# The last 96 rows of an FFN product in 32-row tiles of the array, four token tiles at a time

## The chip, the cores and the metric

The kernel runs on one core of a Trainium2 chip. A core has a matrix engine (TensorE, PE in the profile; its weight loads are listed apart as PEld), three elementwise engines (VectorE or DVE, ScalarE or ACT, GpSimd or POOL) and SyncE (SP), which here only issues DMAs. The engines run side by side and wait for each other by semaphores; each takes its own instructions in the order in which they were written. Matrix products go to PSUM, eight banks of 128 partitions by 512 float32 columns. The metric is the device time of one execution in microseconds, the median of several runs; a profile shows one execution.

## The reference

For 2048 tokens of width 512 the output is a gated sum of two branches:

```python
g = sigmoid((x * gate_w).sum(-1, keepdims=True))
return g * A(x) + (1 - g) * B(x)
# A: q, k, v = x @ wqkv in 32 heads of 16;  pq = q @ w_phi, pk = k @ w_phi, head by head
#    phi(p) = concat(softmax(p), softmax(-p))
#    kv = sum_s phi_k^T v,  z = sum_s phi_k;  o = (phi_q kv) / (phi_q z);  A = o @ wo
# B: relu(x @ w1) @ w2, inner width 1376
```

The inner width 1376 is ten blocks of 128 and a remainder of 96. The change is about that remainder.

## The kernel before, in words

The 2048 tokens are 16 tiles `m` of 128 (NT), or four chunks `c` of 512. All instructions are added as named tasks with their dependencies, and the strings in `ORDER` (line 17) fix by hand the order in which each engine runs its tasks. A task waits until its dependencies are done, and what stands behind it on its engine waits with it. Figures such as `dur` and `boost` in the code belong to a planner and set nothing here.

The tasks that matter:

- `h{c}_{k}` (line 391): first FFN product for chunk c and hidden block k, written transposed (hidden rows, token columns); `rl{c}_{k}` on ScalarE applies ReLU and writes it into `HT` (line 469). For the remainder, k = 10, `h{c}_10` (line 399) computes 97 columns for each of four token tiles, tokens in rows: 96 hidden columns and the gate's product. `rl{c}_10` writes the 96 into `HR` (line 452), and a DMA transpose `hx{c}` on SP brings four blocks of 128 by 128 into `HT` (line 454). `hpad` (line 251) clears the columns 96 to 127.
- `f1_{j}`, `fe1_{j}`, j = 0 to 3: the feature map folded into the key projection's weights, on TensorE, and its copy out of PSUM, on VectorE (j even) and ScalarE (j odd).
- `pr_k0` to `pr_k8`, then `pr_q0` to `pr_q8` (line 512): key and query projections into PSUM banks 0 and 1, two token tiles at a time (the last two of each kind one). Each is followed by a chain through the elementwise engines: `ev` (copy, ScalarE), `mx` and `mn` (VectorE), `t1` and `t2` (GpSimd), `ex` (exponential, ScalarE), `sm` and `rc` (sum and reciprocal, VectorE), `ra` and `nm` (GpSimd).
- `v{m}`, `kv{m}`: values and the sums over keys. `kn`, `kz`: the masked copies of those sums.
- `tq{m}`: DMA transpose of the normalised query features. `nd{m}_0`, `nd{m}_1` (line 616): four small matmuls each, numerator and denominator of tile m, into bank 6 and bank 7. `rd{m}_*` and `o{m}_*` (lines 623, 625): reciprocal and quotient on VectorE; an `o` frees the bank, so `nd2_0` waits for `o1_0`. `to{m}`: DMA transpose of the quotient.
- `b{m}` (line 638): the second FFN product of tile m, eleven matmuls of 512 columns into one of the banks 3, 4, 5, 2 (`AB`, tile m takes the entry m modulo 4), the last with 96 rows. It leaves the accumulation open. `a{m}` (line 644): four matmuls with `wo` that end it. The quotient was scaled by exp of the gate's sum, so that one factor 1 - g serves both.
- `oe{m}` (line 689): multiplies by 1 - g and copies out of PSUM, on ScalarE; it frees the bank for `b{m+4}`. `st{m}`: the store, from ScalarE's queue. Tile 15 is computed in two column parts, `b15` (line 659) for both, then `a15_0`, `a15_1` (line 670), with copies on ScalarE (line 677) and VectorE (line 680).

The loads stand at the head of SP's queue: `w2a` and `w2b` are the ten full blocks of `w2` and its last 96 rows, `wo` the output weights.

Of the kernel before, what the change touches and what calls it, by code (L numbers as in the profile page):

```python
# [5 lines left out]
ACT = mybir.ActivationFunctionType  # L6
ALU = mybir.AluOpType
# [14 lines left out]
    ),  # L22
# [15 lines left out]
    ),  # L38
# [11 lines left out]
    ),  # L50
# [10 lines left out]
    ),  # L61
# [87 lines left out]
def bass_gated_mix__linear_kernel_hedgehog__dense_activation_relu__prompt_kernel(  # L149
# [32 lines left out]
    NDB, AB = (6, 7), (3, 4, 5, 2)  # L182
    GATE_LIMIT = 40.0
    WARM = (6 * (512,),)
    RL = 400.0
    FE = "dve"

    with ExitStack() as es:
        E = es.enter_context

        def sb(name, shape, dt):
            return E(nc.sbuf_tensor(name, shape, dt))

        XT = sb("XT", [P, ND, S], BF16)
        HT = sb("HT", [P, KT, S], BF16)
        WT = sb("WT", [P, 2 * ND, D], BF16)
        WP = sb("WP", [P, 2, ND, D], BF16)
        WV = sb("WV", [P, ND, D], BF16)
        W1 = sb("W1", [P, ND, W1C], BF16)
        W2 = sb("W2", [P, KT, D], BF16)  # L200
        WO = sb("WO", [P, ND, D], BF16)
        WPS = sb("WPS", [P, ND, DH], BF16)
# [30 lines left out]
        EPS = 8 * 512  # L233

        def ap(t, row, off, dims):
            return bass.AP(tensor=t, offset=off, ap=[[row, P]] + [list(d) for d in dims])

        def psap(off, dims):
# [11 lines left out]
            ap(VS, NT * NG * GZ, GV, [[GZ, NT * NG], [1, 1]]), 1.0), dur=0.7, boost=-1e4)  # L250
        add("hpad", "pool", lambda q: q.memset(HR[:, :, :, KREM:P], 0.0), dur=0.6, boost=-1e4)
        XN = FT[:, NF - 2, :].rearrange("p (m d) -> p m d", d=D)
# [61 lines left out]
        load("w2a", "sp", W2[:, 0:KT - 1, :], B_w2[0:(KT - 1) * P, :].rearrange("(j p) n -> p j n", p=P), dur=0.5, lat=8.0)  # L314
        load("w2b", "sp", W2[0:KREM, KT - 1, :], B_w2[(KT - 1) * P:DFF, :], dur=0.5, lat=8.0)
        load("wo", "sp", WO[:, :, :], A_wo.rearrange("(j p) n -> p j n", p=P), dur=0.5, lat=8.0)

# [124 lines left out]
        for n, (kind, a, k) in enumerate(units):  # L442
            b = GB4[n] if n < 4 else FB[2] if n == 4 else HB[(n - 4) % len(HB)]
            if kind == "h":
                halved = n < 4
                deps = [*xof[a], *w1of[k], prev, *freed[b]]
                if k == KT - 1:
                    deps.append("gw")
                    add(f"h{a}_{k}", "pe", lambda q, a=a, b=b: pe_h_tail(q, a, b), deps, dur=0.69)
                    prev = f"h{a}_{k}"  # L450
                    hrow = psap(b * 512, [[KREM + 1, 4], [1, KREM]])
                    add(f"rl{a}_{k}", "act", lambda q, a=a, i=hrow: q.activation(
                        HR[:, a % 2, :, 0:KREM], i, ACT.Relu), (prev, f"hx{a - 2}" if a > 1 else None), dur=0.6, boost=RL)
                    add(f"hx{a}", "sp", lambda q, a=a: q.dma_start_transpose(
                        out=HT[:, KT - 1, chunk(a)].rearrange("p (n t) -> p n t", t=P),
                        in_=HR[:, a % 2, :, :].rearrange("p n k -> p (n k)")),
                        (f"rl{a}_{k}", "hpad"), dur=1.2, lat=1.6, dma=True)
                    add(f"gr{a}", "dve", lambda q, a=a, b=b: q.tensor_scalar(
                        GL[:, 4 * a:4 * a + 4], psap(b * 512 + KREM, [[KREM + 1, 4]]), GATE_LIMIT, -GATE_LIMIT,
                        ALU.min, ALU.max), (prev, f"rl{a}_{k}"), dur=0.2, boost=500.0)  # L460
                    freed[b] = (f"rl{a}_{k}", f"gr{a}")
                    gate(a)
                    continue
# [32 lines left out]
        for m in range(NT):  # L496
            def add(*a, boost=20.0 * (len(widths) * 2 - m // 2 - VLAG), **how):
                return g.add(*a, boost=boost, **how)
# [9 lines left out]

        def pe_proj(q, s, tiles):
            for n, m in enumerate(tiles):  # L510
                for j in range(ND):
                    last = q.matmul(PS[:, n, :], XT[:, j, m * P:(m + 1) * P], WP[:, s, j, :],  # L512
                                    start=(j == 0), stop=(j == ND - 1))
            return last

        jname = []
        for jn, (kind, tiles) in enumerate(jobs):
# [15 lines left out]
            def old(x, J2=two):  # L533
                return f"{x}_{J2}" if J2 else None

            add(f"pr_{J}", "pe", lambda q, s=s, tiles=tiles: pe_proj(q, s, tiles),
                [*(f"fe{s}_{j}" for j in range(ND)), *(d for m in tiles for d in xof[m // 4]),
                 *([f"ev_{before}"] if before else ["fe1_0", "fe1_1"])], dur=0.87 * w)
# [40 lines left out]
            else:  # L579
# [29 lines left out]
                for m in tiles:  # L609
# [25 lines left out]
                    def pe_b(q, m=m, ab=ab):  # L635
                        for k in range(KT):
                            r = P if k < KT - 1 else KREM
                            last = q.matmul(PS[:, ab, :], HT[0:r, k, m * P:(m + 1) * P], W2[0:r, k, :],  # L638
                                            start=(k == 0), stop=False)
                        return last  # L640
# [8 lines left out]
                    if m == NT - 1:  # L649

                        hb = (ab, 0)
                        cols = [slice(0, 352), slice(352, D)]
                        last_b = f"b{m}"

                        def pe_bh(q, m=m, hb=hb, cols=cols):
                            for b, cs in zip(hb, cols):
                                for k in range(KT):
                                    r = P if k < KT - 1 else KREM
                                    last = q.matmul(PS[:, b, 0:cs.stop - cs.start], HT[0:r, k, m * P:(m + 1) * P], W2[0:r, k, cs],  # L659
                                                    start=(k == 0), stop=False)  # L660
                            return last

                        g.add(last_b, "pe", pe_bh, ("w2a", "w2b", *(f"rl{m // 4}_{k}" for k in range(KT - 1)), f"hx{m // 4}", *war,
                                                    f"ev_{J}"), dur=2.42)
                        for h2 in range(2):
                            b, cs = hb[h2], cols[h2]

# [5 lines left out]

                            add(f"a{m}_{h2}", "pe", pe_ah, (last_b, "wo", f"to{m}", f"a{m}_0" if h2 else None), dur=0.44)
                            need = (f"a{m}_{h2}", f"go{m // 4}", f"st{m - NOS}")
# [10 lines left out]
                        continue  # L686
                    g.add(f"b{m}", "pe", pe_b, ("w2a", "w2b", *(f"rl{m // 4}_{k}" for k in range(KT - 1)), f"hx{m // 4}", *war), dur=2.38)
                    add(f"a{m}", "pe", pe_a, (f"b{m}", "wo", f"to{m}"), dur=0.87)
                    add(f"oe{m}", "act", lambda q, m=m, ab=ab: q.activation(  # L689
                        OSB[:, m % NOS, :], PS[:, ab, :], ACT.Copy, scale=OMG[:, m:m + 1]),  # L690
                        (f"a{m}", f"go{m // 4}", f"st{m - NOS}" if m >= NOS else None), dur=0.69)
                    add(f"st{m}", "act", lambda q, m=m: q.dma_start(
                        out=o2[m * P:(m + 1) * P, :], in_=OSB[:, m % NOS, :]), (f"oe{m}",), dur=0.5, lat=1.5, dma=True)
# [44 lines left out]
```

## Time and profile before

| | us |
|---|---|
| median of 3 runs | 150.46 (150.14 to 150.74) |
| profiled execution | 150.59 |
| its span, first to last instruction | 149.3 |
| TensorE busy in it | 146.3 |
| VectorE, GpSimd, ScalarE busy | 110.9, 109.6, 91.8 |

TensorE's granted clock was 1.00 throughout. In the lists of the profile a group is a line of the kernel, an engine, an operation and its tiles (written <- read, buffer numbers left out), with the number of instructions, the time that the group keeps its engine busy, the mean of one in ns, and the engine's idle time just before them with what ended it. The chain in order of time gives start, length and the instructions that it follows. A timeline gives start, length from the first start to the last end, engine, line and shape, and the idle time ahead. W1 and W2 share the name W.

### The profile page before, as it was taken

The page shows a single profiled execution, that of the slowest core. Times are in us where ns is not written, and L with a number is a line of the kernel's source. Part 1 is how long each engine was busy: PE and PEld are TensorE (multiplying, and loading weights), DVE is VectorE, ACT ScalarE, POOL GpSimd, SP SyncE. Part 2 cuts the span into 40 slices and gives each one's busy share as a digit, 9 for nine tenths or more (in the row PEclk, how much of TensorE's full clock was granted, in tenths as well). Part 3 has the DMA queues.
Part 4 walks back from the last instruction along what each step waited for, and adds up shares of the span by engine and source line. Part 5 has one row for each costly group of instructions (what it writes and reads, how often), then busy time and mean ns, then how long its engine had stood idle before and what let it go on. Part 6 is the DMA issues. An engine that isn't in the chain of part 4 may idle for free.

```text
span 149.3 us, 2619 instructions
## 1 busy us (share of the span) xinstructions
PE 146.3 (98%) x1009; PEld 75.9 (51%) x1009; DVE 110.9 (74%) x168; ACT 91.8 (61%) x127; POOL 109.6 (73%) x72
## 2 busy tenths in 40 slices
PE   7999999999999999999999999999999999999994
PEld 2865444444754465445444545455444444445452
DVE  2343666999796948989999997999989988534401
ACT  3374769799979775898983937175573751310151
POOL 4000399999999999999999999999999793150000
PEclk9999999999999999999999999999999999999999
DMA  5999999900030001000000094646778687656552
GB/s 144 303 234 247 171 212 211 341 27 0 7 70 0 0 4 37 0 0 4 0 0 0 2 111 104 141 103 139 121 169 190 159 212 97 156 134 159 63 156 91
DMA packets 46364, 16.11 MB, mean 108 GB/s; under 512 B 39856, under 2 KB 46352, under 8 KB 46352
## 3 DMA queue, kind: packets, MB, share of 16 engines
q1 hardware_dynamic: 43616, 13.50, 43.2%
q10 hardware_dynamic: 2736, 2.45, 5.1%
q8 instruction: 8, 0.13, 0.4%
q14 instruction: 4, 0.03, 0.1%
HBM read 4.41 MB, written 2.10 MB: 44 GB/s over the span
## 4 chain that ended last, share of the span: by engine, by line
PE 98%; DVE 0%; issue 0%
PE PS L638 24%; PE PS L391 21%; PE PS L512 19%; PE PS L492 9%; PE PS L644 9%; PE PS L573 3%; PE PS L616 3%; PE PS L399 2%; PE PS L405 2%; PE PS L258 2%; PE PS L659 2%; PE PS L411 1%; PE PS L374 1%; PE PS L350 1%; PE PS L670 1%; DVE OSB L680 0%
## 5 line engine op out<-in xcount | busy, mean ns | idle before, releaser
L552 POOL TENSOR_TENSOR TS<-PB,MX 128x1024 bf16<-128x1024 bf16 (+1 forms) x18 | 30.9, 1723 | 15.0 <-DVE MX L543 15.0
L638 PE MATMUL PS<-W,HT 128*128 128x512 bf16 (+1 forms) x165 | 38.1, 379 | 0.0
L559 DVE TENSOR_REDUCE ZB<-FT 128x128 f32<-128x2048 bf16 (+1 forms) x18 | 36.6, 2031 | 1.8 <-ACT FT L557 1.8
L557 ACT ACTIVATE FT<-TS 128x2048 bf16<-128x2048 bf16 (+1 forms) x18 | 30.9, 1718 | 8.7 <-POOL TS L552 8.5
L391 PE MATMUL PS<-XT,W 128*128 128x512 bf16 x144 | 34.7, 379 | 0.0
L552 POOL TENSOR_TENSOR TS<-MN,PB 128x1024 bf16<-128x1024 bf16 (+1 forms) x18 | 30.9, 1725 | 0.8 <-DVE MN L545 0.8
L512 PE MATMUL PS<-WP,XT 128*128 128x512 bf16 x128 | 30.6, 379 | 0.0
L566 POOL TENSOR_TENSOR FT<-FT,SC 128x2048 bf16<-128x2048 bf16 (+1 forms) x9 | 29.5, 3287 | 0.0
L469 ACT ACTIVATE HT<-PS 128x512 bf16<-128x512 f32 x40 | 22.6, 597 | 5.6 <-PE PS L391 4.6
L638 PEld LDWEIGHTS PS<-W,HT 128*128 128x128 bf16 (+1 forms) x165 | 15.5, 98 | 17.1
L689 ACT ACTIVATE OSB<-PS,OMG 128x512 bf16<-128x512 f32 x15 | 10.2, 687 | 22.4 <-PE PS L644 22.3
L543 DVE TENSOR_REDUCE MX<-PB 128x64 bf16<-128x1024 bf16 (+1 forms) x18 | 19.5, 1084 | 6.0 <-ACT PB L539 6.0
L545 DVE TENSOR_REDUCE MN<-PB 128x64 bf16<-128x1024 bf16 (+1 forms) x18 | 19.3, 1084 | 3.2 <-ACT PB L539 3.2
L391 PEld LDWEIGHTS PS<-XT,W 128*128 128x128 bf16 x144 | 13.8, 98 | 15.3
L539 ACT ACTIVATE PB<-PS 128x1024 bf16<-128x1024 f32 (+1 forms) x18 | 16.7, 927 | 7.3 <-PE PS L512 4.2
L512 PEld LDWEIGHTS PS<-WP,XT 128*128 128x128 bf16 x128 | 12.0, 98 | 13.6 <-DVE WP L344 0.4
L492 PE MATMUL PS<-WV,XT 128*128 128x512 bf16 x64 | 16.4, 379 | 0.0
L589 POOL TENSOR_TENSOR FT<-FT,SR 128x1024 bf16<-128x1024 bf16 (+1 forms) x9 | 15.7, 1739 | 0.7
L644 PE MATMUL PS<-WO,OT 128*128 128x512 bf16 x60 | 14.7, 379 | 0.0
L625 DVE SCALAR_TENSOR_TENSOR OTM<-PS,EG,RD 128x256 bf16<-128x256 f32 x32 | 13.8, 463 | 0.4 <-DVE RD L623 0.2
L623 DVE RECIPROCAL RD<-PS 128x16 f32<-128x16 f32 x32 | 6.4, 232 | 9.0 <-PE PS L616 8.8
L501 ACT ACTIVATE VS<-PS 128x512 bf16<-128x512 f32 x16 | 9.6, 602 | 4.3 <-PE PS L492 4.3
(54 smaller groups left out, 106.0 us busy)
## 6 DMA issues: line engine op xcount, KB each, us to landing
out_dram<-OSB ACTq DMA_DIRECT2D x15, 128.0 KB, 2.1
W<-in_B_w_dram SPq DMA_DIRECT2D x1, 1280.0 KB, 6.9
W<-in_B_w_dram SPq DMA_DIRECT2D x1, 512.0 KB, 4.9
WV<-in_A_wqkv_dram SPq DMA_DIRECT2D x1, 512.0 KB, 4.7
WO<-in_A_wo_dram SPq DMA_DIRECT2D x1, 512.0 KB, 7.2
FT<-in_A_x_dram SPq DMA_DIRECT2D x3, 128.0 KB, 3.8
W<-in_B_w_dram SPq DMA_DIRECT2D x1, 352.0 KB, 3.9
W<-in_B_w_dram ACTq DMA_DIRECT2D x2, 128.0 KB, 3.7
```

What stands on the lines that cost most here:

```text
L391: last = q.matmul(PS[:, b, :], W1[:, j, k * P:(k + 1) * P], XT[:, j, chunk(c)], start=(j == 0), stop=(j == ND - 1))
L469: add(f"rl{a}_{k}", "act", lambda q, a=a, k=k, b=b: q.activation(HT[:, k, chunk(a)], PS[:, b, :], ACT.Relu), (prev,), dur=0.6, boost=RL)
L492: last = q.matmul(PS[:, 2, :], XT[:, j, m * P:(m + 1) * P], WV[:, j, :], start=(j == 0), stop=(j == ND - 1))
L512: last = q.matmul(PS[:, n, :], XT[:, j, m * P:(m + 1) * P], WP[:, s, j, :], start=(j == 0), stop=(j == ND - 1))
L543: add(f"mx_{J}", "dve", lambda q, sl=sl, w=w, i=pbg: q.tensor_reduce(MX[:, sl, 0:w * H], i, AX.X, ALU.max), (f"ev_{J}", old("t1")), dur=0. ...
L545: add(f"mn_{J}", "dve", lambda q, sl=sl, w=w, i=pbg: q.tensor_reduce(MN[:, sl, 0:w * H], i, AX.X, ALU.min), (f"ev_{J}", old("t2")), dur=0. ...
L552: add(f"{tn}_{J}", "pool", lambda q, o3=o3, a3=a3, b3=b3: q.tensor_tensor(o3, a3, b3, ALU.subtract), (f"{'mx' if sg == 0 else 'mn'}_{J}", ...
L557: add(f"ex_{J}", "act", lambda q, fs=fs, ts=ts, w=w: q.activation(FT[:, fs, 0:w * F], TS[:, ts, 0:w * F], ACT.Exp), (f"t1_{J}", f"t2_{J}", ...
L559: add(f"sm_{J}", "dve", lambda q, fs=fs, sl=sl, w=w: q.tensor_reduce(ZB[:, sl, 0:2 * w * H], FT[:, fs, 0:w * F].rearrange("p (g d) -> p g ...
L566: add(f"nm_{J}", "pool", lambda q, f3=f3, sl=sl, w=w: q.tensor_tensor(f3, f3, SC[:, sl, 0:2 * w * H].unsqueeze(2).to_broadcast([P, 2 * w * ...
L638: last = q.matmul(PS[:, ab, :], HT[0:r, k, m * P:(m + 1) * P], W2[0:r, k, :], start=(k == 0), stop=False)
L644: last = q.matmul(PS[:, ab, :], OT[:, m % NOT, t, :], WO[:, t, :], start=False, stop=(t == ND - 1))
```

## The change

For token tiles 0 to 11 the last 96 rows leave the eleven-matmul product, which becomes ten. They are computed for four token tiles at once: a pack `p{c}`, c = 0, 1, 2, has 3 x 4 matmuls, each with 32 rows of the array. Row tile r (partitions 32r to 32r+31) holds token tile 4c + r and writes that tile's own bank. For this, `rl{c}_10` writes the remainder interleaved, so that one transposed block holds 32 hidden rows of each of the four token tiles (three blocks for each chunk; chunk 3 keeps four blocks and the old form); they go to a new buffer `HX`. The last 96 rows of `w2` are loaded four times more, by `w2x0` to `w2x3`, once for each row tile, into `W2X`. The order is rewritten: a pack follows the `b` of its four tiles, and the `a` tasks follow the pack. `pr_k0` is parted: its first two matmuls, `pr_k0a`, wait for the first two folded weights alone. Tile 15's columns are parted 416 and 96 in place of 352 and 160, its two parts are separate tasks, and `a14` stands between them; `oe14` moves to VectorE, `st14` to SP.

The order on TensorE, from `b0` on, as far as it differs:

```diff
-b0 nd0_0 nd0_1 b3 nd1_0 nd1_1 b2 pr_q6 a0 nd2_0 nd2_1 b1 nd3_1 pr_q7 nd3_0 b4 ...
+b0 nd0_0 nd0_1 b3 nd1_0 nd1_1 b2 pr_q6 nd2_0 nd2_1 b1 p0 a0 nd3_1 pr_q7 nd3_0 b4 ...
-b5 nd6_0 nd6_1 b7 nd7_0 nd7_1 a4 a5 b6 nd8_1 nd8_0 a6 b9 ...
+b5 nd6_0 nd6_1 b7 nd7_0 nd7_1 b6 p1 a4 a5 nd8_1 nd8_0 a6 b9 ...
-b10 nd11_1 a8 nd11_0 a9 b11 a10 nd12_0 nd12_1 b13 ...
+b10 nd11_1 nd11_0 b11 p2 a8 a9 a10 nd12_0 nd12_1 b13 ...
-a11 a12 a13 a14 b15 a15_0 a15_1
+a11 a12 a13 b15_0 a14 a15_0 b15_1 a15_1
```

On the other queues: SP has `w2x0 w2x1 w2x2 w2x3` between `w2b` and `wo`, and `st14` ahead of `st15_1`; ScalarE has `oe4` (with `oe5`, `oe6` behind it) after `ex_q6 gp2` in place of before `oe5 ge2 st2 ex_q6 gp2`, and no `oe14` and `st14`; VectorE has `oe14` between `o15_1` and `oe15_1`. VectorE's and GpSimd's orders are otherwise the same. The code, cut to its core:

```diff
+    NR = KREM // 32
-        HT = sb("HT", [P, KT, S], BF16)
+        HT = sb("HT", [P, KT - 1, S], BF16)
+        HX = sb("HX", [P, NC, 4 * P], BF16)
+        W2X = sb("W2X", [P, NR, D], BF16)
+        def ht(r, k, m):
+            if k == KT - 1:
+                return HX[0:r, m // 4, (m % 4) * P:(m % 4 + 1) * P]
+            return HT[0:r, k, m * P:(m + 1) * P]
...
-        add("hpad", "pool", lambda q: q.memset(HR[:, :, :, KREM:P], 0.0), dur=0.6, boost=-1e4)
+        add("hpad", "pool", lambda q: q.memset(HR[:, 1, :, KREM:P], 0.0), dur=0.6, boost=-1e4)
...
+        for n in range(4):
+            load(f"w2x{n}", "sp", W2X[32 * n:32 * n + 32, :, :], B_w2[(KT - 1) * P:DFF, :].rearrange("(f p) n -> p f n", p=32),
+                 dur=0.5, lat=8.0)
...
+                    nb = NR if a < NC - 1 else 4
+                    if nb == NR:
+                        hi = psap(b * 512, [[KREM + 1, 4], [32, NR], [1, 32]])
+                        ho = ap(HR, 8 * P, (a % 2) * 4 * P, [[32, 4], [P, NR], [1, 32]])
+                    else:
+                        hi = psap(b * 512, [[KREM + 1, 4], [1, KREM]])
+                        ho = HR[:, a % 2, :, 0:KREM]
+                    add(f"rl{a}_{k}", "act", lambda q, o=ho, i=hi: q.activation(o, i, ACT.Relu),
+                        (prev, "hpad", f"hx{a - 2}" if a > 1 else None), dur=0.6, boost=RL)
+                    add(f"hx{a}", "sp", lambda q, a=a, nb=nb: q.dma_start_transpose(
+                        out=HX[:, a, 0:nb * P].rearrange("p (n t) -> p n t", t=P),
+                        in_=HR[:, a % 2, 0:nb, :].rearrange("p n k -> p (n k)")),
...
+            steps = [(n2, m, j) for n2, m in enumerate(tiles) for j in range(ND)]
+            if jn == 0:
+                add(f"pr_{J}a", "pe", lambda q, s=s, steps=steps[:2]: pe_proj(q, s, steps),
+                    [f"fe{s}_0", f"fe{s}_1", *xof[0]], dur=0.44)
+                steps = steps[2:]
...
-                        for k in range(KT):
+                        for k in range(KT if m >= 12 else KT - 1):
                             r = P if k < KT - 1 else KREM
-                            last = q.matmul(PS[:, ab, :], HT[0:r, k, m * P:(m + 1) * P], W2[0:r, k, :],
+                            last = q.matmul(PS[:, ab, :], ht(r, k, m), W2[0:r, k, :],
                                             start=(k == 0), stop=False)
...
-                        cols = [slice(0, 352), slice(352, D)]
+                        cols = [slice(0, 416), slice(416, D)]
...
+                    if m < 12 and m % 4 == 0:
+
+                        def pe_p(q, c=m // 4):
+                            for f in range(NR):
+                                for r in range(4):
+                                    rows = slice(32 * r, 32 * r + 32)
+                                    last = q.matmul(PS[:, AB[r], :], HX[rows, c, f * P:(f + 1) * P], W2X[rows, f, :],
+                                                    start=False, stop=False)
+                            return last
+
+                        g.add(f"p{m // 4}", "pe", pe_p, (*(f"w2x{n}" for n in range(4)), f"hx{m // 4}"), dur=0.75)
+                    add(f"a{m}", "pe", pe_a, (f"b{m}", f"p{m // 4}" if m < 12 else None, "wo", f"to{m}"), dur=0.87)
...
+                        add(f"oe{m}", "dve", lambda q, m=m, ab=ab: q.tensor_scalar(
+                            OSB[:, m % NOS, :], PS[:, ab, :], OMG[:, m:m + 1], None, ALU.mult), need, dur=0.75)
+                    add(f"st{m}", "act" if m < NT - 2 else "sp", lambda q, m=m: q.dma_start(
```

More of the change, by code (lines that the diff above doesn't have):

```diff
@@ L450, in bass_gated_mix__linear_kernel_hedgehog__dense_activation_relu__prompt_kernel @@
                     prev = f"h{a}_{k}"
[L451 to L457, printed above, removed]
+                    nb = NR if a < NC - 1 else 4
[10 more added lines that the diff above has]
+                        in_=HR[:, a % 2, 0:nb, :].rearrange("p n k -> p (n k)")),
+                        (f"rl{a}_{k}",), dur=1.2, lat=1.6, dma=True)
                     add(f"gr{a}", "dve", lambda q, a=a, b=b: q.tensor_scalar(
@@ L507, in bass_gated_mix__linear_kernel_hedgehog__dense_activation_relu__prompt_kernel, with pe_proj @@
         kind_n = {"k": 0, "q": 0}
[L509 to L513, printed above, removed]
+        def pe_proj(q, s, steps):
+            for n, m, j in steps:
+                last = q.matmul(PS[:, n, :], XT[:, j, m * P:(m + 1) * P], WP[:, s, j, :],
+                                start=(j == 0), stop=(j == ND - 1))
             return last
@@ L534, in old @@
                 return f"{x}_{J2}" if J2 else None
-            add(f"pr_{J}", "pe", lambda q, s=s, tiles=tiles: pe_proj(q, s, tiles),
-                [*(f"fe{s}_{j}" for j in range(ND)), *(d for m in tiles for d in xof[m // 4]),
+            steps = [(n2, m, j) for n2, m in enumerate(tiles) for j in range(ND)]
[3 more added lines that the diff above has]
+                steps = steps[2:]
+            add(f"pr_{J}", "pe", lambda q, s=s, steps=steps: pe_proj(q, s, steps),
+                [f"pr_{J}a" if jn == 0 else None, *(f"fe{s}_{j}" for j in range(ND)), *(d for m in tiles for d in xof[m // 4]),
                  *([f"ev_{before}"] if before else ["fe1_0", "fe1_1"])], dur=0.87 * w)
@@ L651, in bass_gated_mix__linear_kernel_hedgehog__dense_activation_relu__prompt_kernel, with pe_bh @@
                         hb = (ab, 0)
-                        cols = [slice(0, 352), slice(352, D)]
-                        last_b = f"b{m}"
-                        def pe_bh(q, m=m, hb=hb, cols=cols):
-                            for b, cs in zip(hb, cols):
+                        cols = [slice(0, 416), slice(416, D)]
+                        prev = None
+                        for h2 in range(2):
+                            b, cs = hb[h2], cols[h2]
+                            def pe_bh(q, m=m, b=b, cs=cs):
                                 for k in range(KT):
                                     r = P if k < KT - 1 else KREM
-                                    last = q.matmul(PS[:, b, 0:cs.stop - cs.start], HT[0:r, k, m * P:(m + 1) * P], W2[0:r, k, cs],
+                                    last = q.matmul(PS[:, b, 0:cs.stop - cs.start], ht(r, k, m), W2[0:r, k, cs],
                                                     start=(k == 0), stop=False)
[L661 to L666, printed above, removed]
+                                return last
+                            last_b = f"b{m}_{h2}"
+                            g.add(last_b, "pe", pe_bh, ("w2a", "w2b", *(f"rl{m // 4}_{k}" for k in range(KT - 1)), f"hx{m // 4}", *war,
+                                                        f"ev_{J}", prev), dur=1.2)
+                            prev = f"a{m}_{h2}"
                             def pe_ah(q, m=m, b=b, cs=cs):
@@ L672, in pe_ah @@
                                 return last
-                            add(f"a{m}_{h2}", "pe", pe_ah, (last_b, "wo", f"to{m}", f"a{m}_0" if h2 else None), dur=0.44)
+                            add(f"a{m}_{h2}", "pe", pe_ah, (last_b, "wo", f"to{m}"), dur=0.44)
                             need = (f"a{m}_{h2}", f"go{m // 4}", f"st{m - NOS}")
@@ L686, in bass_gated_mix__linear_kernel_hedgehog__dense_activation_relu__prompt_kernel @@
                         continue
[L687 to L692, printed above, removed]
+                    tail = ("w2b", f"hx{m // 4}") if m >= 12 else ()
+                    g.add(f"b{m}", "pe", pe_b, ("w2a", *(f"rl{m // 4}_{k}" for k in range(KT - 1)), *tail, *war), dur=2.38)
+                    if m < 12 and m % 4 == 0:
[5 more added lines that the diff above has]
+                                                    start=False, stop=False)
+                            return last
+                        g.add(f"p{m // 4}", "pe", pe_p, (*(f"w2x{n}" for n in range(4)), f"hx{m // 4}"), dur=0.75)
+                    add(f"a{m}", "pe", pe_a, (f"b{m}", f"p{m // 4}" if m < 12 else None, "wo", f"to{m}"), dur=0.87)
+                    need = (f"a{m}", f"go{m // 4}", f"st{m - NOS}" if m >= NOS else None)
+                    if m < NT - 2:
+                        add(f"oe{m}", "act", lambda q, m=m, ab=ab: q.activation(
+                            OSB[:, m % NOS, :], PS[:, ab, :], ACT.Copy, scale=OMG[:, m:m + 1]), need, dur=0.69)
+                    else:
+                        add(f"oe{m}", "dve", lambda q, m=m, ab=ab: q.tensor_scalar(
+                            OSB[:, m % NOS, :], PS[:, ab, :], OMG[:, m:m + 1], None, ALU.mult), need, dur=0.75)
+                    add(f"st{m}", "act" if m < NT - 2 else "sp", lambda q, m=m: q.dma_start(
                         out=o2[m * P:(m + 1) * P, :], in_=OSB[:, m % NOS, :]), (f"oe{m}",), dur=0.5, lat=1.5, dma=True)
```

20 rows, old and new, of the table ORDER are left out of this document.

## The prediction

> **What bounds the kernel now.** I read the page's busy shares and its chain first, then the chain in order of time, then the timelines of TensorE and VectorE around the place that the new order rearranges, then the queues. From the page, busy shares and the chain:
>
> ```profile
> PE 146.3 (98%) x1009; PEld 75.9 (51%) x1009; DVE 110.9 (74%) x168; ACT 91.8 (61%) x127; POOL 109.6 (73%) x72
> ...
> PE 98%; DVE 0%; issue 0%
> ```
>
> TensorE is the bound from the first microsecond to the last: only work taken off it, or an idle stretch put into it, moves the end. But GpSimd runs beside it as a second chain, with next to no gap once it has begun (the groups by line and shape):
>
> ```profile
> L552 POOL TENSOR_TENSOR TS<-PB,MX 128x1024 bf16<-128x1024 bf16 x14 | 26.7, 1915 | 15.0 <-DVE MX L543 15.0
> ...
> L616 PE MATMUL PS<-KVN,PHQ 128*128 128x68 bf16 x128 | 7.2, 194 | 0.0
> ...
> L638 PE MATMUL PS<-W,HT 96*128 96x512 bf16 x15 | 5.7, 381 | 0.0
> ```
>
> Its 15.0 us are the one wait at the start; in 92 to 97 us it is busy 4.92 of 5.00. What hangs on GpSimd cannot come earlier when TensorE hurries. The chain in order of time, at two places:
>
> ```profile
> 13.05 1.84 PE PS L512 x8
> ...
> 92.71 2.38 PE PS L638 x11
> 95.09 1.73 PE PS L512 x8
> 96.82 0.86 PE PS L644 x4
> 97.68 0.26 PE PS L616 x8
> ```
>
> Eleven matmuls of an FFN tile take 2.38 us, 0.2162 us each (a record lasts 0.379: its last 0.163 runs beside the next matmul), and the 96-row one is no shorter. Eight small ones of L616 take 0.26, 0.032 each: as fast as a weight load and a matmul follow each other. Next TensorE's timeline, records by their start, and VectorE's:
>
> ```profile
> 92.55 2.54 PE L638 MATMUL PS<-W,HT 128*128 128x512 bf16 x11
> 94.93 1.89 PE L512 MATMUL PS<-WP,XT 128*128 128x512 bf16 x8
> 96.65 1.03 PE L644 MATMUL PS<-WO,OT 128*128 128x512 bf16 x4
> 97.52 0.42 PE L616 MATMUL PS<-KVN,PHQ 128*128 128x68 bf16 x8
> ```
>
> ```profile
> 92.26 2.29 DVE L559 TENSOR_REDUCE ZB<-FT 128x128 f32<-128x2048 bf16 x1 [0.86 <-ACT FT L557]
> 94.46 0.36 DVE L623 RECIPROCAL RD<-PS 128x16 f32<-128x16 f32 x2
> 94.74 0.49 DVE L583 RECIPROCAL SC<-ZB 128x64 f32<-128x64 f32 x1
> 95.15 1.16 DVE L543 TENSOR_REDUCE MX<-PB 128x64 bf16<-128x1024 bf16 x1
> 96.23 0.86 DVE L625 SCALAR_TENSOR_TENSOR OTM<-PS,EG,RD 128x256 bf16<-128x256 f32 x2
> ```
>
> The matmuls at 97.52 are `nd2_0` and `nd2_1`. They write PSUM banks 6 and 7, which VectorE frees by the last line shown, `o1_1` and `o1_0`, ending at 97.09. These stand in VectorE's queue behind a reduction that waits for ScalarE's exponential, which waits 3.2 us for GpSimd. So `nd2_0` comes only some 0.3 us after its bank is free.
>
> **The change, part by part.**
>
> *Removed:* the 96-row matmul of token tiles 0 to 11: 12 x 0.2162 = 2.59 us of TensorE.
>
> *Added:* three packs `p0` to `p2`, each 12 matmuls of 32 rows by 512 columns. Nothing before has 32 rows. Below, if the four row tiles stream together, a pack is three streams, 3 x 0.2162 = 0.65, and the fourth tile starts three pairs of 0.032 late: 0.745. Above, if they run one after another, it is 12 x 0.2162 = 2.59. Between lies what happens at the borders: ordinary matmuls overlap 0.163 us of their tails, and the trace does not show whether a matmul may enter an array that is still finishing another division; that is none, one or two tails, 0.745, 0.91 or 1.07. I take one, 0.91, the middle of the case in which the packs do what they say: 3 x 0.91 = 2.73. Removal and packs together cost +0.14; they pay only below 0.865 us a pack, since 36 quarter-height matmuls are worth nine full ones against twelve.
>
> Two sentences from the Trainium skill. "TensorEngine Tiling (Array Packing)", Key Properties, says that a change of tiling mode drains TensorE: that would be both tails, 1.07 a pack and 0.48 more in sum. "TensorE: Matmul & The Clock Gate", Part 3, gives 3.07x for four row tiles: by that an estimate of 12 x 0.2162 / 3.07 = 0.845 a pack, 0.20 less in sum. No trace so far shows either.
>
> *First key projection.* Its first matmul starts at 13.01, where TensorE was free at 12.885 (`h0_6`, four from 12.02): it waits for all four folded weights. With `pr_k0a` on the first two alone it starts at once: -0.125 us. As this releases GpSimd's first operation, the second chain moves 0.125 earlier too, but no more.
>
> *The order around `p0`.* A pack accumulates into four open banks, so `a0` must follow it; `pr_q6` is now followed by `nd2_0` directly. Ahead of `nd2_0`, TensorE loses `a0` (0.865), three 96-row matmuls (0.65) and 0.125: 1.64 us. It arrives at 97.52 - 1.64 = 95.88. Its bank is free at 97.09 - 0.125 = 96.97, and the way from a VectorE end to the first matmul is 0.17 (fold casts ending at 12.84, matmul at 13.01): 97.135. TensorE idles 1.25 us, between 1.1 (no such lag) and 1.3. `a0` was the cover and is gone. Everything behind on TensorE's queue is late by it: `b1`, `p0`, `a0`, `nd3_1`, `pr_q7`, `nd3_0`, `b4`.
>
> *Who waits next.* VectorE's `rd3_0` waits for `nd3_0`, about 1.2 us later than before; so `rc_q3`, GpSimd's `ra_q3` and the chain behind it slip by about a microsecond. That is covered: the last phase transposes issue near 134 us and their matmuls come at 139.9. In before `a3` waits 0.14 for the transpose `to3`, which took 4.0 us from issue to landing against a median of 2.4. Both move back alike; I take the median landing, which removes the wait (-0.14), and keep up to +0.3 if the long landing stays. `b4` then follows `oe0` by under 0.1 us, as `b9` follows `oe5` and `b13` `oe9`: ScalarE needs 0.04 + 0.69 + 0.17 after an output product, TensorE has 0.96 to 0.99 of cover. I cost these at nothing, up to 0.1 each. Packs 1 and 2 shift output products behind phase matmuls whose banks were free for 0.5 us or more.
>
> *Queues.* Four `w2x` loads on SP, some 0.62 us of issue each as the two W2 loads (1.23), stand ahead of `wo` and `hx0`. SP is idle from 24.2 to 40.2, so 2.5 us hide; `wo`, landing 7 us after issue, is wanted at 97. The transposes of the remainder shrink from four blocks to three; half a 0.63 us memset on GpSimd goes in its idle start; the remainder's ReLU writes as many elements (0.51). All nothing. ScalarE's `oe4` behind `ex_q6` still ends before `b8` needs its bank by over 2 us.
>
> *The end.* 416 and 96 columns in place of 352 and 160 is the same number of columns, and 97-column matmuls (L399) already keep 0.043 us each: zero on TensorE. `a14` now runs between the halves and ends well before; `oe14` on VectorE (0.69, as the 512-column casts) is over 0.6 us before `oe15_1`. The last copy shrinks from 160 columns, 0.384, to 96; on the line through 0.384 and 0.688 that is 0.33: -0.05. The last store lands 1.73 us after issue as before; `st14` is issued later and shares the queue, up to +0.1.
>
> **The sum:** -2.59 + 2.73 - 0.125 + 1.25 - 0.14 - 0.05 = +1.07 us. The profiled execution takes 150.59 (span 149.3, and 1.3 around it), so 151.66; against the median of the runs, 150.46, it is 151.5.
>
> **Rivals.**
> 1. *The wait before `nd2_0` is not there.* It vanishes if `o1_0` ends 1.25 us sooner, by 95.7. For it: VectorE idles 0.86 before this stretch. Against: that idle time ends with GpSimd, which has no gap. The sum is then -0.18, 150.3, not slower; and with no tails (0.745) -0.67, 149.8. It becomes faster by over 0.5% below about 0.72 a pack.
> 2. *Both tails are exposed,* 1.07 a pack: +1.55, 152.0. For it: each pack has two borders where matmuls of other height meet. Against: 96-row matmuls between 128-row ones cost nothing. It is what the Trainium skill's page "TensorEngine Tiling (Array Packing)", Key Properties, would make of it.
> 3. *The row tiles run one after another,* so the change doesn't do what it says: 3 x 1.68 more, +6.1, 156.6; two by two, 1.30 a pack, 152.7. For it: 96 rows take as long as 128. Against: they write different banks from different rows.
>
> **How the numbers follow.** About 0.5%, 0.75 us, is what a measurement here can tell from no change. The forecast (the wait, none to nearly two tails) has 0.58; its own range is 150.8 to 152.1, of which about 0.14 lies within 0.75 us (no tail: +0.57) and 0.44 above. Rival 1 has 0.20, 0.11 of it faster and 0.09 the same; rival 2 has 0.14, rival 3 0.08, both slower. That makes faster 0.11, same 0.23, slower 0.66. A range of 150.0 to 152.6 holds the forecast, rival 2 and half of rival 1, and leaves out rival 3 and the faster part of rival 1.
>
> **What would show it.** In TensorE's timeline: no gap before L512 at 13; an idle stretch of some 1.2 us ahead of the L616 matmuls of tile 2, released by VectorE's OTM; three packs of twelve 32-row records, each 0.75 to 1.07 us from its first start to the next matmul's; GpSimd idle by about a microsecond near 102; ten matmuls in 2.16 us. The prediction is wrong if the phase matmuls follow `pr_q6` without a gap, if the packs take over 1.1 us or under 0.7, or if the loads on SP delay a transpose.

## The result and the profile after

| | before | after |
|---|---|---|
| median, us | 150.29 (6 runs, 150.14 to 150.74) | 151.50 (6 runs, 150.94 to 151.64) |
| profiled execution, us | 150.59 | 151.64 |
| its span, us | 149.3 | 149.9 |
| outside the span, us | 1.29 | 1.74 |

The kernel before has three more runs here than in the first part. The ratio is 1.007, 95% interval 1.005 to 1.0089: slower, by 0.7%. A little over half of the microsecond lies within the span; the rest lies outside it, where no list of the profile reaches.

The page of the changed kernel, busy shares and chain:

```profile
PE 145.0 (97%) x1016; PEld 74.9 (50%) x1033; DVE 111.4 (74%) x169; ACT 91.4 (61%) x126; POOL 109.4 (73%) x72
...
POOL 47%; PE 43%; issue 5%; DVE 3%; ACT 1%; POOLq 0%
```

Seventeen matmul records are missing here (1016 against 1033 weight loads). The chain has changed hands: followed back from the end it is TensorE's only as far as 97 us, and before that GpSimd's. The chain in order of time shows the place:

```profile
92.49 1.88 POOL TS L573
94.37 0.01 issue
94.38 0.15 DVE RD L644
94.53 0.01 issue
94.55 0.20 DVE RD L644
94.74 0.41 DVE SC L604
95.15 1.08 DVE MX L564
96.23 0.79 DVE OTM L646 x2
97.02 0.14 issue
97.16 0.41 PE PS L637 x8
97.57 2.16 PE PS L659 x10
99.73 0.76 PE PS L717 x12
```

L637 are the phase matmuls (`nd2`), L646 the quotients (`o1`), L659 a `b` with ten matmuls, L717 a pack. The same stretch in TensorE's timeline:

```profile
94.19 1.89 PE L528 MATMUL PS<-WP,XT 128*128 128x512 bf16 x8
97.16 0.41 PE L637 MATMUL PS<-KVN,PHQ 128*128 128x68 bf16 x8 [1.08 <-DVE OTM L646]
97.41 2.32 PE L659 MATMUL PS<-W,HT 128*128 128x512 bf16 x10
```

The eight matmuls of `pr_q6` start at 94.19 and fill 8 x 0.2162 us, to 95.92. `nd2_0` starts at 97.16: 1.24 us of TensorE with nothing in them (the profile writes 1.08, as it counts from the modelled end of the last record). The release is `o1_0`, which ends at 97.01.

The first pack, weight loads and matmuls, and the first matmul behind it:

```profile
99.66 0.34 PEld L717 LDWEIGHTS PS<-W2X,HX 32*128 32x128 bf16 x12 [0.42 <-issue]
99.66 0.82 PE L717 MATMUL PS<-W2X,HX 32*128 32x512 bf16 x12
100.42 1.04 PE L665 MATMUL PS<-WO,OT 128*128 128x512 bf16 x3
```

The twelve records start in three groups of four, 2 to 4 ns apart within a group, the groups 0.216 to 0.226 us apart. `b1`, from 97.41 with ten matmuls, would have let the next one in at 99.57; the pack comes at 99.66, 0.09 late, and the matmul behind it 0.31 after the pack's last start where 0.216 would do, again 0.09 late. From 99.57 to 100.42 a pack is 0.855 us; the other two agree within 1 ns.

Start of the same task after, less before:

| task | us |
|---|---|
| `kv15`, just ahead of `b0` | -0.08 |
| `b4`, behind the wait, `p0` and the moved `a0` | +1.14 |
| `nd5_0`, and `b5` two tasks later | +0.92, +0.76 |
| `nd12`, behind the last pack | +0.95 |
| last copy, `oe15_1` | +0.95 |
| end of the span | +0.6 |
| time | +1.05 |

At the very end the changed kernel wins something back. VectorE's last copy and the last store, in the timeline:

```profile
148.03 0.32 DVE L702 TENSOR_SCALAR OSB<-PS,OMG 128x96 bf16<-128x96 f32 x1 [0.59 <-PE PS L692]
148.38 0.36 SPq L705 DMA_DIRECT2D out_dram<-OSB  x1
```

The copy takes 0.32 us against 0.38, and the store lands 1.48 us after its issue against 1.73 (24 KB against 40 KB): 0.31 us less from TensorE's end to the end of the span.

### The profile page after: what moved, and what is told of

The parts are those of the page before. It is cut to its first block, busy times and chain, and to the rows that moved or that the text cites. A ratio compares the mean times of both kernels' runs of the same rounds, so it can differ in the third digit from the quotient of the medians.

```text
span 149.9 us, 2654 instructions
## 1 busy us (share of the span) xinstructions
PE 145.0 (97%) x1016; PEld 74.9 (50%) x1033; DVE 111.4 (74%) x169; ACT 91.4 (61%) x126; POOL 109.4 (73%) x72
## 4 chain that ended last, share of the span: by engine, by line
POOL 47%; PE 43%; issue 5%; DVE 3%; ACT 1%; POOLq 0%
POOL TS L573 28%; PE PS L659 18%; POOL FT L587 16%; PE PS L665 9%; POOL FT L610 3%; PE PS L637 2%; PE PS L528 2%; PE PS L416 2%; PE PS L266 2%; PE PS L402 2%; PE PS L681 2%; DVE MX L564 2%; PE PS L717 2%; PE PS L422 1%; PE PS L361 1%
## 5 line engine op out<-in xcount | busy, mean ns | idle before, releaser
L659 PE MATMUL PS<-W,HT 128*128 128x512 bf16 x148 | 34.4, 379 | 0.1
L528 PE MATMUL PS<-WP,XT 128*128 128x512 bf16 x124 | 29.9, 379 | 0.2
L725 ACT ACTIVATE OSB<-PS,OMG 128x512 bf16<-128x512 f32 x14 | 9.6, 687 | 22.2 <-PE PS L665 21.6
L659 PEld LDWEIGHTS PS<-W,HT 128*128 128x128 bf16 x150 | 13.9, 98 | 14.9 <-ACT OSB L725 0.2
L509 PE MATMUL PS<-WV,XT 128*128 128x512 bf16 x61 | 15.8, 379 | 0.2
L665 PE MATMUL PS<-WO,OT 128*128 128x512 bf16 x55 | 13.8, 379 | 0.4 <-issue 0.2
L646 DVE SCALAR_TENSOR_TENSOR OTM<-PS,EG,RD 128x256 bf16<-128x256 f32 x32 | 13.8, 463 | 0.2
```

Of the source, the lines that this page charges most:

```text
L659: last = q.matmul(PS[:, ab, :], ht(r, k, m), W2[0:r, k, :], start=(k == 0), stop=False)
L665: last = q.matmul(PS[:, ab, :], OT[:, m % NOT, t, :], WO[:, t, :], start=False, stop=(t == ND - 1))
```

## The experiments

In each, "before" and "changed" are the two kernels of the front part; the ratios are to runs of the kernel before beside it on the same chip. "Outside" is the time less the span, the median over the runs.

**1. The cover put back.**

```diff
-b2 pr_q6 nd2_0 nd2_1 b1 p0 a0 nd3_1 ...
+b2 pr_q6 b1 nd2_0 nd2_1 p0 a0 nd3_1 ...
```

> The changed kernel with one edit in TensorE's order: nd2_0 and nd2_1 come after b1 in place of before it, so that ten matmuls (2.16 us) cover the wait for o1_0. Theory (the wait of 1.24 us before nd2_0 is TensorE time lost for good): nd2_0 starts near 98.1, no gap before it; VectorE's rd2_0 is some 0.35 us later than in the changed kernel; the end moves by -1.0 to -1.25 us, span near 148.8, and the time is some 1.1 us below the changed kernel's 151.5, level with the kernel before (150.3). Rival (GpSimd's chain is the bound by now, and the wait only shows at another place when it is taken away here): nd3 or a3 waits in its stead, and the time stays at 151.3 to 151.5.

Measured: ratio 1.0016 [0.9991, 1.0042], 150.78 against 150.51; spans of its runs 149.05 us in the median, where the changed kernel's had 149.8. TensorE's timeline around the place, in this kernel:

```profile
94.36 1.89 PE L528 MATMUL PS<-WP,XT 128*128 128x512 bf16 x8
96.09 2.32 PE L659 MATMUL PS<-W,HT 128*128 128x512 bf16 x10
98.25 0.42 PE L637 MATMUL PS<-KVN,PHQ 128*128 128x68 bf16 x8
98.59 0.83 PE L717 MATMUL PS<-W2X,HX 32*128 32x512 bf16 x12
```

No gap: each task begins where the one ahead leaves off, but for 0.09 us ahead of the pack. Its last matmul ends at 147.04, 0.95 us ahead of the changed kernel's. Of the 1.24 us, 0.17 are missing because this execution was late by that much before the place (`kv15` starts at 87.12 against 86.94), and 0.10 come back as a wait of `a3` for its transpose; nothing else does. So it was lost time and not slack that GpSimd holds anyway. By the ratios (1.007 and 1.0016), one exchange of two tasks buys back 0.8 us of the 1.05. What is left against the kernel before lies outside the span: 1.73 us against 1.31, while the spans are 149.05 against 149.2.

**2. The order alone, without packs.** In the kernel before:

```diff
-b2 pr_q6 a0 nd2_0 nd2_1 b1 nd3_1 ...
+b2 pr_q6 nd2_0 nd2_1 b1 a0 nd3_1 ...
```

> The kernel before, with one edit in TensorE's order: a0 moves behind b1, no packs, nothing else. Theory (the order makes the wait, not the packs): TensorE arrives at nd2_0 at 97.52 - 0.865 = 96.65, the bank is free for it at 97.26: a gap of 0.6 us, and 0.4 to 0.6 us more time than the kernel before, 150.7 to 150.9. Rival (the packs or their 32-row mode make the wait): no gap and no change.

Measured: ratio 1.0037 [1.0014, 1.006], 0.55 us. The profiled execution began 0.34 us late and also met a slow transpose near its end, so only the stretch itself is read from it, in TensorE's timeline:

```profile
95.27 1.89 PE L512 MATMUL PS<-WP,XT 128*128 128x512 bf16 x8
97.57 0.41 PE L616 MATMUL PS<-KVN,PHQ 128*128 128x68 bf16 x8 [0.41 <-DVE OTM L625]
```

From 95.27 + 1.73 = 97.00 to 97.57 are 0.57 us of idle TensorE, released by the same quotient. The order alone makes a wait; it needs neither the packs nor their row tiles. The other 0.67 of the 1.24 fits the three 96-row matmuls (0.65 us) that the changed kernel no longer has ahead of `nd2_0`.

**3. A pack in another order.** In the changed kernel:

```diff
-                            for f in range(NR):
-                                for r in range(4):
+                            for r in range(4):
+                                for f in range(NR):
```

> The changed kernel with the pack's two loops exchanged: the three matmuls of one row tile follow each other, then those of the next, so that only neighbours in the order can stream together. Theory (four row tiles stream side by side only when they follow each other; matmuls start in order): a pack takes 4 x 2 x 0.216 + 0.216 + 0.18 = 2.1 us against 0.86, so 3 x 1.27 = 3.8 us more, 155.3. Rival (a pack's time does not hang on the order of its matmuls, because the array takes any that is ready): 151.5.

Measured: ratio 1.008 [1.0051, 1.011], 151.54: as the changed kernel. My theory falls. TensorE's timeline:

```profile
98.73 0.38 PE L659 MATMUL PS<-W,HT 128*128 128x512 bf16 x1
99.04 0.85 PE L717 MATMUL PS<-W2X,HX 32*128 32x512 bf16 x12
99.82 0.39 PE L665 MATMUL PS<-WO,OT 128*128 128x512 bf16 x1
```

The pack is 0.78 us from its first start to the next task's, against 0.76. Again four records start together, now 9 to 11 ns apart in place of 2 to 4. That is about three times the step, as it would be if three pairs of weight load and matmul were handed out for each start. The records do not name the row tile; the next experiment closes that.

**4. Twelve matmuls in one row tile.** In the changed kernel; the rest of the remainder is left out:

```diff
-                                    rows = slice(32 * r, 32 * r + 32)
+                                    rows = slice(0, 32)
```

> The changed kernel with all twelve matmuls of a pack in the first row tile (rows 0 to 31); the products of the other three row tiles' rows are left out, so that three tokens tiles of each four get a wrong remainder. Theory (a row tile is a stream of its own, 0.216 us for each matmul, and only different row tiles run side by side): 12 x 0.216 + 0.18 = 2.77 us a pack, 3 x 1.92 = 5.7 us more than the changed kernel, about 157. Rival (32-row matmuls are started without regard to their rows): 0.86 us a pack as before.

Measured, one execution: 159.12 us; TensorE's timeline:

```profile
99.66 2.76 PE L717 MATMUL PS<-W2X,HX 32*128 32x512 bf16 x12
102.35 0.60 PE L665 MATMUL PS<-WO,OT 128*128 128x512 bf16 x2
```

All twelve start 0.216 us after one another (the first step 0.226), and with the 0.09 at entry the pack is 2.78 us: the expected 2.77. So one row tile is one stream, and a 32-row matmul costs as much as a 128-row one. The time is 1.9 us above what the longer packs account for. Most of that lies behind the second pack, and it is no idle stretch: the granted clock in the page of this run falls there,

```profile
PEclk9999999999999999999999999999998799999999
```

and from 120.4 to 123.8 us its mean is 0.51. The matmuls of `a4` and `a5` start 0.427 us apart in place of 0.216, which costs 1.67 us. Why the clock fell is not shown. Together with experiment 3 this settles more: as the matmuls of one row tile start 0.216 us apart, then, if all started strictly in order, three of one row tile in a row would hold up the next tile, and the pack of experiment 3 could not be under 8 x 0.216 + 0.216 = 1.94 us. It was 0.78. The row tiles run past one another.

**5. The end alone.** The kernel before with columns 416 and 96, `b15_0` and `b15_1` apart and `a14` between, `oe14` on VectorE, `st14` on SP:

```diff
-a11 a12 a13 a14 b15 a15_0 a15_1
+a11 a12 a13 b15_0 a14 a15_0 b15_1 a15_1
...
-                        cols = [slice(0, 352), slice(352, D)]
+                        cols = [slice(0, 416), slice(416, D)]
...
```

> The kernel before with the change's end alone: columns 416 and 96, two separate parts of tile 15 with a14 between them, oe14 on VectorE and st14 on SP. Theory (from the changed kernel's trace, the stretch from TensorE's end to the span's end is 0.3 us shorter: a copy of 0.32 in place of 0.38 and a last store of 1.48 in place of 1.73 us): 0.2 to 0.35 us less than before, span near 149.0, 150.1 to 150.3 where before is 150.5. Rival (the store's landing is chance, only the smaller copy counts): 0.05 us less.

Measured: ratio 0.9984 [0.9962, 1.0006], not clear of no change. Its spans are 148.6 us in the median against 149.0 for the kernel before beside it: 0.4 us won where the profile looks. Outside the span lie 1.68 us against 1.33 in the median, with no extra load at all. But this median hides two levels: of the twelve executions of this one program, five have 1.29 to 1.38 us outside, as the kernel before, and seven 1.66 to 1.85.

**6. The end and the parted key projection.** As experiment 5, and:

```diff
-h0_6 pr_k0 h0_7
+h0_6 pr_k0a pr_k0 h0_7
...
```

> The kernel before with the parted first key projection and the change's end; no packs, no extra loads, order around the output products as before. Theory (the parts of the change add up): 0.3 to 0.45 us less than before, 150.05 to 150.2 where before is 150.5. Rival (the time saved at pr_k0 is lost again where TensorE waits for what GpSimd releases): no more saved than by the end alone.

Measured: ratio 0.9984 [0.9963, 1.0004]; spans 148.65, outside 1.77 in the median; here too there are two levels, three executions at 1.31 to 1.37 and nine at 1.70 to 1.90. In its trace `pr_k0a` starts without a gap and the chain behind it comes 0.12 us earlier against its own start phase (0.15 late ahead of `pr_k0`, 0.03 late behind it). The runs cannot tell a tenth from nothing.

**7. The four loads alone.** The kernel before with `w2x0` to `w2x3` on SP and waited for by `b0`:

```diff
-... gw w2a w2b wo hx0 ...
+... gw w2a w2b w2x0 w2x1 w2x2 w2x3 wo hx0 ...
...
```

> The kernel before plus the four loads of the last 96 rows of w2 into their own buffer, at the same place on SP's queue and waited for by b0; nobody reads what they bring. In the changed kernel's profiled execution 1.74 us lie outside the span, in that of the kernel before 1.29. Theory (the 0.45 us come with the four loads and their semaphores): span unchanged at 149.3, time 150.6 to 150.8. Rival (they come from elsewhere, such as the end, where the last stores are issued on other queues): span and time unchanged, 150.2 to 150.4.

Measured: ratio 1.004 [1.0015, 1.0065], 0.55 us. Spans 149.35 against 149.2; outside 1.73 against 1.31. The four loads cost 0.4 us outside; the 0.15 us between the spans are within the scatter of the runs, so no cost on the core's engines shows, as forecast.

**8. Four loads, one semaphore.**

```diff
+                if t.name.startswith("w2x"):
+                    t.sem, t.count = "w2x", 64
...
```

> The kernel before plus the four loads of e4, their data unread, but all four counting on one semaphore in place of four. Outside the span the kernel before has 1.3 us, the one with four loads on four semaphores 1.73. Theory (each further semaphore costs 0.11 us outside the span): 1.40. Rival (each further DMA does): 1.73.

Measured, one execution: 1.77 us outside. It does not take four semaphores.

**9. Thirty-two semaphores fewer.** The kernel before with

```diff
+                ring = {"tq": 7, "to": 4, "st": 5}.get(t.name[:2])
+                if ring and t.name[2:].isdigit() and t.dma:
+                    m = int(t.name[2:])
+                    t.sem, t.count = f"{t.name[:2]}{m % ring}", 16 * (m // ring + 1)
...
```

> The kernel before, with semaphores used again: the transposes tq in turn on seven, to on four, the stores st on five, counting on; 32 semaphores fewer, 32 fewer to be waited for by name, no other edit. Theory (0.11 us outside the span for each semaphore): outside near zero if it went on so far, and at most 1.3 us less; span unchanged. Rival (the number of semaphores sets nothing, or only past a certain number): 1.3 us outside, 150.5.

Measured: ratio 1.0004 [0.9981, 1.0028], 1.32 us outside. No effect at all.

**10. Waits in place of DMAs.** The kernel before with

```diff
         for m in range(NT - NOS - 2, NT - 1):
             nc.sync.wait_ge(sems[f"st{m}"], 16)
+        for n in range(4):
+            nc.sync.wait_ge(sems[f"st{n}"], 16)
```

> The kernel before with four more waits at the end of SyncE's program, on stores that have long landed; no DMA is added. So far the time outside the span is 1.3 us with 55 DMAs on SP's queue and 1.7 with 56 or more, whatever else differs. Theory (the number of DMAs on that queue sets it): 1.3 us outside. Rival (the length of SyncE's program sets it): 1.7.

Measured, one execution: 1.64 us outside. Four instructions that wait for nothing and move nothing, added to SyncE's program, bring most of it in this execution; the kernel before stayed between 1.27 and 1.38 in all 86 executions beside the experiments. So it does not take a DMA either.

**11. The end with `st14` left on ScalarE.** Experiment 6 with

```diff
-                    add(f"st{m}", "act" if m < NT - 2 else "sp", lambda q, m=m: q.dma_start(
+                    add(f"st{m}", "act", lambda q, m=m: q.dma_start(
...
```

> The kernel before with the parted first key projection and the change's end, but with st14 left on ScalarE's queue, so that SP has its 55 DMAs again. Theory (what lies outside the span goes by SP's queue): 1.3 us outside, span 148.6 to 148.9, 150.0, 0.3 to 0.4 us less than before. Rival (it goes by something else in the end part): 1.7 outside and no gain beyond 0.15.

Measured: ratio 0.9987 [0.9964, 1.001], 150.35 against 150.47; outside 1.33, as the theory had it, and 1.27 to 1.39 in all twelve executions, but the spans are 149.0 against 149.15. With `st14` ahead of it on ScalarE's queue, `oe15_0` starts 0.55 us after TensorE has finished its part, and its store lands last. What is won outside is lost within.

**12. The change repaired.** Experiment 1's order, the loads on ScalarE's queue after `rl3_10`, `st14` on ScalarE:

> The changed kernel, repaired: nd2 behind b1, the four extra loads on ScalarE's queue after rl3_10 (its idle stretch from 87 to 90 us), st14 on ScalarE's queue. SP has 55 DMAs. Theory (the wait, SP's queue and nothing else made the change slower; a pack costs 0.856 us against 0.865): 1.3 us outside, and within 0.1 us of e10_k0a_end_act, which has no packs, about 150.0. Rival (the packs have a gain of their own that the wait hid): 0.4 us or more below e10_k0a_end_act.

Measured: ratio 1.0034 [1.0005, 1.0064], 150.88; outside 1.59, spans 149.3. It is half a microsecond behind experiment 11 and not level with it. About 0.26 us of that is outside the span, although SyncE's program is as long as in the kernel before; here ScalarE's is longer by four DMAs and TensorE's by 24 matmuls. The other 0.3 us in the medians of the spans is not explained; its spans scatter from 148.5 to 150.5, and in its profiled execution TensorE ends at 146.75, ahead of the kernel before. The rival, a hidden gain of the packs, is excluded.

No version tried is clear of the kernel before on the fast side. The nearest are experiments 5 and 6, 0.16% below it with intervals that reach past 1.

## Why the prediction was right, and where by luck

The forecast was 151.5, and 151.5 came; the sum was +1.07 on the profiled execution, and +1.05 came. Its main term was right for the reason given. Others were not, and they cancel: the sum had the packs and the end 0.43 us too dear and left out the 0.45 us outside the span. That the total came out so close is luck. The medians moved by more than the profiled executions: from 150.29 to 151.50, +1.21.

| term | forecast | measured | where |
|---|---|---|---|
| wait before `nd2_0` | +1.25 | +1.24 | gap from 95.92 to 97.16; experiments 1 and 2 |
| removed rows and packs | +0.14 | -0.03 | 3 x 0.855 - 2.59 |
| first key projection | -0.125 | -0.08 | start of `kv15` |
| wait of `a3` | -0.14 | -0.16 | +0.92 at `nd5_0`, +0.76 at `b5` |
| end | -0.05 | -0.31 | copy -0.06, store -0.25 |
| outside the span | 0 | +0.45 | experiments 5, 7, 10 |
| sum | +1.07 | +1.1 | time +1.05 |

*The wait.* Every step held: that GpSimd's chain does not move, that `o1_0` follows from it through ScalarE and VectorE, that `a0` and the three shorter `b` brought TensorE there 1.6 us sooner, that the way from VectorE to the matmul is under 0.2. Nothing behind it gave the time back but the 0.16 at `a3`, as TensorE had no other idle time to give. That VectorE, GpSimd and the transposes slip along, covered, is right too: `rd3_0` came 1.05 us later, GpSimd's `ra_q3` 1.06, and GpSimd stood idle for 1.11 us from 102.25. The loads on SP delayed no transpose of the remainder: `hx0` was issued at 40.15 us against 40.23. `to3` landed 3.1 us after its issue, later than the 2.4 that I took but sooner than the 4.0 before, and `a3` did not wait, as forecast.

*The first key projection.* The step held: the gap is gone, and `pr_k0a` starts 0.86 us after `h0_6` where `pr_k0` took 0.98. The 0.12 shows as 0.08 at `kv15` because this execution reached `h0_6` 0.04 late.

*The packs.* The step "none, one or two tails of 0.163" took the wrong size: both borders cost something, 0.09 us each, 0.18 together, and the three streams 0.67. The pack is 0.855 us where I took 0.91, in the range of 0.745 to 1.07 and on its break-even of 0.865: the packs are worth 0.03 us in all. The Trainium skill, "TensorEngine Tiling (Array Packing)", Key Properties, has a change of tiling mode drain TensorE; the trace agrees that the border costs, at 0.09 us, a little over half of the 0.163 that I took for a full drain. The Trainium skill, "TensorE: Matmul & The Clock Gate", Part 3, gives 3.07x for four row tiles, by which an estimate is 0.845 a pack; measured, 12 x 0.2162 / 0.855 = 3.03x.

*The end.* "The last store lands 1.73 us after issue as before" was wrong: 1.48 in the changed kernel, 1.53 in experiment 5, with 24 KB. `st14` did it no harm.

*Outside the span.* "Four `w2x` loads ... All nothing" was right for the engines, but the sum took the 1.3 us around the span for fixed. It is 1.27 to 1.39 us in every execution of the kernel before beside the experiments and of experiments 2, 9 and 11, 1.56 to 1.67 in experiment 12, and 1.64 to 1.77 in the changed kernel and in experiments 1, 3, 4, 7, 8 and 10. Experiments 5 and 6 have one DMA more on SyncE, and one and the same program shows both levels there, the longer one in 16 of 24 executions. So it takes neither further semaphores (8, 9) nor further DMAs (10), and the length of a program alone does not settle it either: experiment 12 has most of it with SyncE's program as long as before, and 5 and 6 change their level from one execution to the next. A longer program on SyncE makes the longer time likely; what sets it stays open.

*The rivals.* The wait was there, so rival 1 falls; without it the measured terms add up to -0.13, near the -0.18 that rival 1 had worked out. Both tails in full, rival 2, fall by the 0.09. Serial row tiles, rival 3, exist if one asks for them: experiment 4 is the 2.6 us pack that it had feared.

## What to carry to other kernels

When one engine is busy throughout and another runs a gapless chain beside it, moving work away from ahead of a wait is not free: look up when the awaited result comes, and keep as much work in front of it as there was. Splitting a remainder into row tiles gains only what the count of streams says (here 36 quarters against 12 wholes, nine streams against twelve, less two borders for each pack): work that out first. Compare time and span separately, and execution by execution; a part of a microsecond can arise where the profile does not look, and a median can hide two levels.

## What the hardware showed that I had not expected

- Row tiles pass each other. With three matmuls of one row tile in succession (experiment 3) the pack took 0.78 us where starting in order would need 1.94; the four tiles began 10 ns apart. So within TensorE matmuls of different row tiles do not start in the order in which they were written, other than the introduction says of the engines. The Trainium skill, "TensorE: Matmul & The Clock Gate", Part 3, calls matmuls strictly first-in, first-out in start and end; this run does not agree.
- The border between 128-row and 32-row matmuls costs 0.09 us each way: the next weight load comes 0.303 to 0.308 us after the last matmul's start, in and out of all three packs, and its matmul 4 to 5 ns later (one such matmul's record is missing).
- The time outside the span has levels: 1.3 us, 1.6 and 1.64 to 1.90. In one execution, four idle waits on SyncE were enough to leave the first; with one DMA more on SyncE (experiments 5 and 6) a program takes the first in 8 of 24 executions and the last in the others.
